# Later loads paced at even distances and a newly searched instruction order in a sparse-attention and gated-FFN kernel

## Chip, cores and metric

The kernel runs on one core of a Trainium2 chip. The metric is device time of one execution in microseconds; three runs of the kernel before took 208.0, 208.16 and 208.38, so its median is 208.16 us. A profile is taken of a further execution.

## What is computed

Block-sparse attention (the mask keeps the window, the first and last blocks, and three drawn blocks for each query block) for 4 batches of 8 heads, 768 tokens of 64 values, and behind it a feed-forward layer whose hidden values are gated by a convolution over three tokens:

```python
scores = scale * np.matmul(q, k.transpose(0, 1, 3, 2))
...
scores = np.where(mask, scores, -1000000000.0)
...
return np.matmul(attn, v).astype(np.float32)      # (4, 8, 768, 64)
...
h = np.maximum(x @ w_in, 0.0)                     # x: (4, 768, 512), w_in: (512, 1024)
...
for k in range(K):
    conv_out += conv_w[k][None, None, :] * hp[:, k:k + S, :]
gate = 1.0 / (1.0 + np.exp(-conv_out))
return (h * gate @ w_out).astype(np.float32)      # w_out: (1024, 512)
```

## The kernel before

**Work.** The 32 heads are taken as 16 pairs, four to a batch. Scores are made transposed, keys on the partitions, in blocks of 128 keys by 128 queries; the mask rides along as 24 extra rows of the contraction (so 88 rows), which is why a pair's slot `t` holds 64 rows of queries and keys and 24 of mask. Eight blocks are one *unit*: score matmuls into a two-bank tile `st` of which there are two (L762), one exponential of 1024 columns on ScalarE into `pt` (L774), and eight matmuls of 65 columns that add up attention times V and its sum in `av` (L799). There are 144 units, 18 for each half of a batch. A pair is thus needed from a known unit on, and comes back in the second half of its batch.

**Behind the scores.** For each half batch and pair, VectorE takes the reciprocal and scales (L707, L709) into `xtok`; a crossbar turn (a transposing DMA on the SP queue, L718) or, at the first and the last pieces, a PE transpose (L728) makes `xT`. The first FFN product (L896) goes through `mix` banks, and is evicted with ReLU into `hE` by ScalarE (L916) or VectorE (L918). The convolution is three products and two sums on VectorE (L954, L962), or for one piece on PE (L973); tanh on ScalarE (L1001, L978) and two more VectorE operations (L1004, L1009) make the gated values `gT`. The second product (L831) is evicted into `o2s` by either engine (the copy helper: L327 on ScalarE, L331 on VectorE) and written out on the SP queue (L840). There are two `mix` banks, and PE's transposes use them too.

**Loads.** Pairs 1 to 5 are loaded by POOL's queue (L239) as natural rows `nat` and `nq` and turned by PE transposes, copied into `t` by the helper. From pair 6 on, K and Q land in `nat`, two crossbar turns on SP (L597) bring them to the staging tile `stg`, and two VectorE copies of 64x1536 bring these into `t` (L331, tile `t<-stg`). V lands in `vn` and is copied to `vt`. Only two staging tiles, four `nat` and three `vn` exist, so a load waits for the copy that empties its buffer.

**Pacing.** POOL would issue every load as soon as a buffer is free. For pairs 8 to 15 a one-element POOL copy (`pace`, L407) reads a corner of the exponential of a chosen unit, so that POOL's queue, which works in order, goes on only once that unit is done. `PACE_U(P)` (L412) gives the unit for K; in `kq_crossbar` and `v_pair` the loads of Q and V follow some units later. Loads of pairs 4 to 7 and of the weights follow each other at a fixed number of loads (L673).

**The order.** Nothing is scheduled when the kernel is built. `Graph` collects 1787 operations, each with its possible engines; `ORDER`, a string of two characters for each operation, one for the engine where there is a choice and one for each buffer that it takes, gives the order in which they are put down, and so the order on every engine and queue. Each engine works through its part in order; waits come from the data and buffers alone.

Of the kernel before, what the change touches and what calls it, by code (L numbers as in the profile page):

```python
# [21 lines left out]
1K11H00l0m0n0o0p0q0Y0Z10V1FA01LA1h0/A1BA1JV0+1GV0r0s0t0u11V1d16V1IA5805910v18V0w0x0y1M05a05b1NV1O01/1262h12j32k  # L22
2v20z0A0B0C0D0E1SA05e05f5j1195g11V15k0F1Y05c05o05p5d0G5l21WV11ZV1+V1XV5q35h0H5t15u0I0J5i5m5C05D5v45H15I2702a1
5E55J05M05N5n5r5s5w5R11b24V11a28V22cV2bV29V5S0K1k15x15F1l1s2iV25y05O15T25+05/5G5K5L5P603631642l0680695Q5U2o1654
5z6d16e6a56f02mV35V2nV2qV2pV5A06i06j1P1610626k16r16s6t25BV01c5W11RV662001QV6w06x676b6c6g5X6y36B16C5Y16h6l6D46G0
6H6I51o1j2wV31n1t6n221V2d22x24S2y5ZV6o6m16u6v6z22V6P16Q6A6E6F6U06V6J6K4T1u6p12r34U2J04V1v2L06R06L06M6W16Z16+6S0
6T6N04W2M4X1w6qV720734Y2X16/27436OV2e1ih0ii4Z1x4+2Z14/2+501y6X1r2KV41p2fV1q2gVijA00771787f07947gik0il6Y707k17h5
7l7m051in1717p07q7r1imViF0iGiHiIio75767u17vipV17w2iq0iriJiK2z17C07D7a7b1isV2AV42BV7H17i7j7I7n7o7s2s0iN17c1iO7E3
7J47t7M07N2C12tV2uViP2EV2DV7x7y7z2iQ7R17S7O57T0iz0iA1z523427AiLiBV27W0537Xit182183iu7F17G7Y1842870887diw0ix7K
8c1iR893ivV37LiS8diyViM02N12OV07P8h08i142PV8e42Q07Q7UiV27V7Z8j53008p18q8r0iW7+085868a3635437557e18u08v8b8fiC1  # L30
8z18A8w1iD2/1317/0iY80382812RV2SViTiXiUiEV8B28g8E08F8k8l8s132V8m18J18K8G3391jf08R08S7B8t8x8y8L48T58W18X8C8D8H8I
8Y08/090911j9194195j138n8oiZj22YV033Vj3j4j58Mjg8N08Ui+962i/8O0j08P3a9c08V8Q28Z8+92939djaj697989h19i9e3jbjhj7992
j89j59a159m09njijc9r19s9o1jdA0jjV13cV3bV3f3g23d0562F03i9w09t41m35V1jo0jpjl1jqA9xjm9y09E13h573o9FjnVjJ0jKjLjMjN
3eV2ju0jv9G29J09K9f19g9k9ljwA9O19p9q9P9L32G1jr02IV2HV9Q59u9T09vjs9UjtV9/19z9A0a03r3s02T13u3p13tjO9V1jR1jS9B1jP
jUjT9CjV9Hjx1jy9IjA0jBa14jzAa40a5jCA2U12VVa919MjZ2a60jW9N9Raaae0jD0jE2WVj+jXafab2ag39SjG1jH9W9Xa21jFA3DjIAaj1ak
ar0a3jQk0j/9Y09Za7a8acaskj0adahal1jYje9b3k03w19D3lkv1aw1ax3j33v4aik1at4k2aB0aCk53k7k6k8k9ay0kwam3E13A3B23Gk3k4
aD5kakbkc9+3xan0kkauavazaAaG1aHaEaFaO0aPklkxaI23nVaQ3aT1aUaV1kmkyknV2ao23yVapaJaY0aZkzA3a+4b11aKb23mVkB0kCkE1kF
kDV14kGVkZ0k+aL1l0aM3F3P3Q33M3S3N03qV33CV4b35b60b7b80be1aR1kK0bfaSbg23R3X3Y1kH1aWkLkMAbj0kIbkaXa/kJA5l51b0b4b5
b93zVbo1bpk/bb0l6l7kN0kObl3bt0bul8bcl1bq1kPA6bv4kQ1bB1kRbCba0bhkW0bibG0bmbHkSAld2lelfbD5bnbrbsbwbxkXbL1bE1bI0l2
aq03I0kojk3T1aN3J3H0bdkAbFbMbN2kYVby2lgbz3OV0lhl9l3l41bQ0kT1bA3UbRkUkVA7ll3lmbJkp0bKbS3bV1bWkqkrksc10c2bObX1la  # L40
bPbTbUbYc61kd1kec7kfbZ0lic343ZV1lnljlolplblklcktA0kgcb0c4ccc5c85cg1c9lqkhA2cd0lrls3+chci2lz0lAlBlClt13LV3KVco0
cpct1culDV1cq3lF0lGb+1b/lHV3VV13WV3/2434041cv1lucy0czlI0lJcD1cacEcecflvcA4cI0cJlKVm10m3m2cjckcl0m4m5cF5cK0lL0lw
lxA3cQ1cRcmcr1cslMlNVlO1lPcV0cWm6cwcxcBcCcGcS3cX1cHc+1c/m7d04lR0cLd30d4lQVm91mamcmb4c4d042d55cN2mdlU1lVlSlTAdb1
cM0lWVm8cOdclX1dg0cTcUlYdhmh2milZVmemkmfmjl+0l/dd0cYcZdl1dm494h4ed1d2d6di2kuc01440cn4a24f4i1dq0drm0AmgmD1d7de1
dn3lEcPdv1dwmx0dfds1dx5dD0dEdjmEdI1dkdodpdtdudJ4q4r14vmlmp3mqmr45msd81mmmtmnd9dF0dymydN0dOdz0dG4gmumodadK2dA0mv
mwdBmFmzdP3dS1dTmAd+046V2d/dU1dHdLdMdQdRdV4se05mBA0e31e44EmG48dC2e80mHV14jdWe9e11e2e50ea34F3mY0mV14n4o04Jed1ee
mWei0ef1dX2dY4bV2mZ47Veje6e7ebeceq1egmXV08m+Vnh0nieherek54tn21nknj4G4u4Bes4ev0ewn3m/04C14kV3n4Vex0eA1eBelem0n0
eteC3eueF0eGn81eH1eN1n9eOen1eon1V9np1nqnsnrntn50n6eS0eTeynaAne1eP4n7Aanx2ezeDeEeIeJeU2lymImCeK0eLnueX1eQ1nfngA
eYf00f14pV34lVnb0ncnyndVbnlnAnF3nHnz4w04mmJ1mKmLmMeRnvepdZkieMf20eZ3nmnBnneVf50f6mNA3mP0fd1eWfef71ff4nGnIno0nJ
4xnwnCe+mQe/mRmSfi0mTA1fjo61o7fk24H4I4P4Q2o30nKnDnEo8AnLfn1o4o5A4yV4fofs0ftfp5fu3ot14zVouov4DA44RV0nMf3f4f8fa1  # L50
f90fgfhnT1flfmnN0nUfA1fBfF0fGnOnVowoxnWfH0fC1nPfK0fqfLnQoyfM4fbnXV0frfvfP1fQfw4K14Lo01nRV24MV04NVfx2fR2ozoAnZ0
n+n/Ao1fU0fVg01g1fD1oc0fEfIfJodo2Aol0omonooopfW5g50g6g23o91oaoeAg71oqobVoB2oDfyoroCosoi0oEga1gbfNfOojfSgf0gc04A
ggof1ogfTgn1fXfY0gog3g4okAohAoR0fZ0nYnSmUoFgh4oX1g8g9gdgp2oJ3f+gs0gtgx1gegigjgq1gyoGoKoLoMoN4Ofc0f/fzoSgu5oYgG0
grgvgz3oHgHgwgAgBgL1gk1oOoIgMgI1oToZgloPoQgN0gQ0gRoUoVA0o+gZ1g+o/V2p70gJ0p8p9papbV1gC0g/4gS2h21gDgmpg1h3phpd0pe
h45h70h8pfA1cpiVh93pm1pnhg1pj0poApkhhgE1gKhl0gOhmgPgTgUh01plAdpB1pCpDpEps0ptpJ0pFgFV1gV2hi1hn0oWp0mOpcpuApGh1h5
hq1pp1pqpKgWpLpMpNprAehrhs2pv0pwpR2pShz0gX1h6hahbhc1hdhj0hAhkhohE1pOgYAhphFhtp11pxAfpPpTpUhB4he0huhv0hfAhG5pHpV
hwp2p3p4py0pI1pzpQhN0p5A0hC1hx1hOhDhHhW1hXhyVqk1pAApWqlhP3hY1qq0qrh/0i0hI0hQhRqmAgpZ3p+pXhJ2q0p/hKq1qsAhq51i81
qB1pYhL0i9qCq2hMA2q6qh0q3hS1qDqEq4hTi10ia2hZ1h+q7qiq8qjAii2i30ibicqn0qFqR0q9A2i40i5i61i7AqoqpAjqGqb1qchU0qt2qu
id2qvhVAqdqwieif0qJ3qKqMqHqxigAqeri0rjqfA3rkAqLqSqyqzr91rarbArA1rBrf0rgrl0rmqArhArc1rdr30qIr4rn2rC1reAqNqOroqT
rpqUqPqQrq0rv1rrrs2rtqVrurR0rL1rwrF1rx3r5rGrSrDryrErzrMrNrOqWrTqaqgp6qXqYr6r7V1rUrPA2rQrVArWr8rHrIrJA3rKqZ0q+q/  # L60
# [53 lines left out]
def kernel(  # L114
# [290 lines left out]
    def pace(u, prio):  # L405
        box = []
        o = op("pace", {"POOL": 0.12}, lambda e: nc.gpsimd.tensor_copy(  # L407
            out=pace_t, in_=pt_t[box[0].index][0:1, 0:1]), prio)
# [649 lines left out]
```

## Time and profile before

| | before |
|---|---|
| runs | 208.0, 208.16, 208.38 us |
| profiled execution | 207.8 us, its span 206.0 us |
| TensorE granted clock | 1.00 throughout |
| read from and written to HBM | 23.09 MB, 6.29 MB |
| DMA, mean over the span | 124 GB/s |

The profile names engines PE (TensorE matmuls), PEld (its weight loads), DVE (VectorE), ACT (ScalarE), POOL and SP. A line of the chain or of the timeline gives start and length in us from the span's start, then engine, tile and source line; an arrow in brackets names what ended the idle time before an instruction. A line of a stretch gives, for each engine, busy us and instructions, then clock, DMA share and GB/s. A line of a wait gives us in total, times, and the longest. Ends of matmuls are modelled, and an engine's durations overlap a little, so distances between starts are the better measure of a rate.

### The profile page before, as it was taken

The numbers are of one execution on the slowest core, as the hardware profiler recorded it, in microseconds if no ns is written. First come the engines' busy times: TensorE is split into PE (matmuls) and PEld (weight loads), VectorE is DVE, ScalarE is ACT, GpSimd is POOL, SyncE is SP. The second block draws the span as 40 slices with busy tenths as digits, with TensorE's granted clock in tenths as the row PEclk, the third lists the DMA queues.
The fourth block names the chain that finished last, engine by engine and source line by source line (L and its number), as shares of the span: only waits on it lengthen the run. The fifth ranks groups of instructions, "written<-read, shape, count | busy, mean of one in ns | idle before, by whom it ended". The sixth has DMA issues, their size and how long they took to land.

```text
span 206.0 us, 6234 instructions
## 1 busy us (share of the span) xinstructions
PE 199.0 (97%) x2409; PEld 142.7 (69%) x2409; DVE 186.3 (90%) x572; ACT 190.5 (92%) x253; POOL 60.7 (29%) x113
## 2 busy tenths in 40 slices
...
GB/s 140 214 196 168 199 154 136 165 123 88 164 129 181 79 191 67 233 149 165 89 59 121 147 110 104 241 149 187 5 165 19 38 175 51 3 2 42 114 28 179
DMA packets 50969, 25.59 MB, mean 124 GB/s; under 512 B 36764, under 2 KB 47996, under 8 KB 50940
## 3 DMA queue, kind: packets, MB, share of 16 engines
...
q14 instruction: 10, 0.08, 0.2%
HBM read 23.09 MB, written 6.29 MB: 143 GB/s over the span
## 4 chain that ended last, share of the span: by engine, by line
PE 76%; ACT 14%; DMA 3%; issue 3%; DVE 2%; SPq 1%; ACTq 0%
PE st L762 26%; PE mix L896 17%; PE mix L831 16%; PE av L799 14%; ACT pt L774 9%; DMA m<-in_v_dram 3%; ACT m L1001 1%; ACT o2s L327 1%; ACT hE L916 1%; PE st L831 1%; PE mix L728 1%; PE mix L522 1%; PE av L973 1%; PE mix L460 1%; DVE t L331 1%
## 5 line engine op out<-in xcount | busy, mean ns | idle before, releaser
L774 ACT ACTIVATE pt<-st 128x1024 bf16<-128x1024 f32 (+1 forms) x145 | 140.2, 1033 | 3.2 <-PE st L762 2.5
L762 PE MATMUL st<-t 88*128 88x256 bf16 (+2 forms) x600 | 91.2, 268 | 1.8 <-DVE t L331 0.9
L762 PEld LDWEIGHTS <-t 88*128 88x128 bf16 x600 | 48.4, 97 | 21.4 <-issue 1.9
L799 PEld LDWEIGHTS <-pt 128*128 128x128 bf16 x1152 | 51.4, 97 | 10.5 <-ACT pt L774 0.2
L799 PE MATMUL av<-vt,pt 128*128 128x65 bf16 x1152 | 57.0, 193 | 0.0
L896 PE MATMUL mix<-xT,winb 128*128 128x384 bf16 (+2 forms) x288 | 54.4, 307 | 0.4 <-ACT o2s L327 0.3
L954 DVE TENSOR_SCALAR m<-hE,cw 128x382 bf16<-128x382 bf16 (+2 forms) x192 | 50.3, 320 | 0.9 <-ACT hE L916 0.6
L831 PE MATMUL mix<-woutb,gT 128*128 128x512 bf16 x184 | 48.5, 379 | 0.0
L962 DVE TENSOR_TENSOR m<-m 128x764 bf16<-128x764 bf16 (+2 forms) x64 | 34.0, 533 | 0.6
L896 PEld LDWEIGHTS <-winb 128*128 128x128 bf16 x288 | 24.7, 97 | 10.2 <-issue 1.3
L1001 ACT ACTIVATE m<-m 128x764 bf16<-128x764 bf16 (+2 forms) x32 | 26.5, 831 | 0.6 <-DVE m L962 0.5
L831 PEld LDWEIGHTS <-gT 128*128 128x128 bf16 x200 | 17.3, 97 | 11.6 <-DVE gT L1009 0.3
L407 POOL COPY pace<-pt 1x1 bf16<-1x1 bf16 x24 | 7.3, 306 | 51.6 <-ACT pt L774 51.5
L916 ACT ACTIVATE hE<-mix 128x384 bf16<-128x384 f32 (+2 forms) x39 | 18.9, 503 | 0.7 <-PE mix L896 0.4
L709 DVE TENSOR_TENSOR xtok<-av,rcp 128x384 bf16<-128x384 f32 (+2 forms) x36 | 18.2, 506 | 0.4
L1009 DVE TENSOR_TENSOR gT<-m,hE 128x764 bf16<-128x764 bf16 (+3 forms) x36 | 18.1, 511 | 0.4
L239 POOL DMA_DIRECT2D nat<-in_q_dram x23 | 17.7, 769 | 1.6 <-issue 1.1
L918 DVE TENSOR_SCALAR hE<-mix 128x384 bf16<-128x384 f32 x25 | 13.7, 552 | 1.0 <-PE mix L896 0.5
L331 DVE COPY t<-mix 64x384 bf16<-64x384 bf16 (+1 forms) x33 | 13.3, 410 | 0.6
L239 POOL DMA_DIRECT2D nat<-in_k_dram x15 | 11.6, 776 | 3.8 <-DMA nat<-in_k_dram 1.8
L1004 DVE TENSOR_SCALAR m<-m 128x764 bf16<-128x764 bf16 (+3 forms) x36 | 12.0, 337 | 0.6 <-ACT m L1001 0.5
L331 DVE COPY o2s<-mix 128x512 f32<-128x512 f32 x9 | 6.2, 688 | 6.5 <-PE mix L831 6.4
...
## 6 DMA issues: line engine op xcount, KB each, us to landing
...
nat<-in_k_dram POOLq DMA_DIRECT2D x15, 192.0 KB, 4.7
vn<-in_v_dram POOLq DMA_DIRECT2D x15, 192.0 KB, 5.8
nat<-in_q_dram POOLq DMA_DIRECT2D x6, 192.0 KB, 5.0
...
```

Of the source, the lines that this page charges most:

```text
L239: return op(name, {eng: occ}, lambda e: on(e).dma_start(out=dst(), in_=src), prio, deps, dma=(kind, service), **kw)
L331: nc.vector.tensor_copy(out=dst, in_=src)
L709: nm = op("norm", {"DVE": t_dps(128 * C)}, lambda e: nc.vector.tensor_tensor(out=xtok_t[xk.index][:, 0:C].rearrange("p c h d -> p h c d"), ...
L762: nc.tensor.matmul(out=st[:, 128 * x:128 * (x + n_)], lhsT=t[0:88, 12 + 6 * hh + kc, :], rhs=t[0:88, idx:idx + (n_ - 1) * (2 if P < NPE el ...
L774: nc.scalar.activation(out=pt_t[ptb.index][:, c0:c1], in_=st_t[stb.index][:, c0:c1], func=AF.Exp, bias=0.0, scale=0.125)
L799: nc.tensor.matmul(out=o[:, off:off + 65], lhsT=pt_t[ptb.index][:, 128 * x:128 * x + 128], rhs=V_t[vslot_b[P].index][:, hh, kc, 0:65], sta ...
L831: nc.tensor.matmul(out=acc(), lhsT=gT_t[gb.index][:, ffc, 128 * t:128 * t + 128], rhs=woutb[:, ffc, c0:c1], start=(ffc == 0), stop=(ffc == ...
L896: nc.tensor.matmul(out=mix_t[hb.index][:, w1 * y:w1 * y + w1], lhsT=winb[:, fc, 128 * ffc:128 * ffc + 128], rhs=xT_t[xt_buf[n].index][:, f ...
L916: nc.scalar.activation(out=dst, in_=src, func=AF.Relu, bias=0.0, scale=0.5)
L954: nc.vector.tensor_scalar(out=m_t[cb.index][:, x, y, 0:w], in0=hE_t[heb.index][:, f0 + y, t0 + x:t0 + x + w], scalar1=cw[:, x, f0 + y:f0 + ...
L962: nc.vector.tensor_tensor(out=m[:, a_, :, 0:w], in0=m[:, a_, :, 0:w], in1=m[:, b_, :, 0:w], op=ALU.add)
L1001: th = [op("tanh", {"ACT": t_act(2 * w) + 0.04}, lambda e, cb=cb, w=w: nc.scalar.activation(out=m_t[cb.index][:, 0, :, 0:w], in_=m_t[cb.in ...
```

## The change

The order string is replaced as a whole. The operations are the same ones, and each keeps its meaning; 28 of them change between ScalarE and VectorE (16 ReLU evictions, 6 output evictions, 2 copies into `xT`, 4 copies and casts of the start). The string was searched with late crossbar turns and late loads among the draws of the search. Beside it, the units that pace the loads of pairs 8 to 15 change: K of the four pairs of a batch at 3, 11, 20, 28 instead of 4, 12, 20, 27 units into the batch before, Q three units behind K instead of two, V six instead of four.

```diff
 ORDER = """
-0002103040M05060708090a011i0L0S0T1T01U2302510b0c0d0e0f1g0U0W0X12V0V1e1f0N0O13A17V0g0h0i0j0k0P0Q0R1AV21CA1DA1E0
...
+000211g010M030405060708090a0S0T1T01U230251262h12j20U0L0O0N0P0Q0R0b0c0d0e0f0g0h0i0j0k0W1e0V0X12V13A17V1AV30Y1CA
...
 """
...
     def PACE_U(P):
         b, j = divmod(P, 4)
-        return 36 * (b - 1) + ((12, 17, 22, 28) if b == 1 else (4, 12, 20, 27))[j]
+        return 36 * (b - 1) + ((12, 17, 22, 28) if b == 1 else (3, 11, 20, 28))[j]
...
-            pq = pace(PACE_U(P) + 2, due - 12)
+            pq = pace(PACE_U(P) + 3, due - 12)
...
-                pv = pace(PACE_U(P) + 4, due - 9)
+                pv = pace(PACE_U(P) + 6, due - 9)
```

More of the change, by code (lines that the diff above doesn't have):

```diff
@@ L20 @@
 ORDER = """
-0002103040M05060708090a011i0L0S0T1T01U2302510b0c0d0e0f1g0U0W0X12V0V1e1f0N0O13A17V0g0h0i0j0k0P0Q0R1AV21CA1DA1E0
[L22 to L60, printed above, removed]
@@ L61 @@
-r0r1A0r2
+000211g010M030405060708090a0S0T1T01U230251262h12j20U0L0O0N0P0Q0R0b0c0d0e0f0g0h0i0j0k0W1e0V0X12V13A17V1AV30Y1CA
+1DA1f1d1E01K10l1H01FA00Z1LV10V0/A0m0n0o0p0q5805911JV1BV1h1GA1IA0r0s0t0u0v1M05a05b0w0x0y0z0A0B0C0D5e05f1NA0+16V
+1SA05j11V15k0E5g15c05d1Y05l211V18V191WV11XV5o05p5q35h1k15i0F1+V1ZV5t15u0G5m0H5n5C05D1O02k1/12d22x31b1a2v21l24V1
+0I0J5r5v45s4S5E55H15I2702a15M05N5J05O10K5R15S5T25w5x15F5G28V22bV2cV29V5+05/5K5L5P6035y02iV21t5z1o631642l1654680
+692o05Q6d16e5U2mV32nV2pV2qV6a55V5A16i06j6f06106266671c5W12y5BV06r16s6k11u1P06b6c4T2r34U2J04V2L04W1v2M6t26w05X6x
@@ new lines @@
+6y36g2016h6B16C6D46l1RV1QV2wV36m16G06H6u1s1n6v6z5Y06I51p4X1w4Y2X14Z1x4+2Z14/2+501y511z5234222V5ZV21V6n26P16Q6R0
+6A6E6F6U06V6J6K1j6o6L06M6p06W16S06Z16+6T6N16qV6OV1r6/2720732e02fV2gV743ih16X77178iiik07f07g794il1q7k17l7h51i
+ijV002KV47m0in16Y707p07q7r1imViF0iGiHiI71ioipV17u17v7w2iJiq0ir7C075762z1isViK2AV42BV7D7H17I7E32C07a7b17i7j7niN1
+7c17J42s17M07N2tV7o7s7t7x537R17S2DV2uV2EViO147y7O57z2iP7AiQiz1iLiR7T03007W07X7Y17diAit082183iBA2842iu870887F17G
+ivV37K7L2N18938c18d7PiM07Q7U7V2OV02PViw07e1iS312/18h0ixiyV8i7Z7+0852Q17/0iV2iW8e48j58p18q3823j38r0868a8b8f8u08v
@@ new lines @@
+2SViT80iYiX8w18g8k8l8z18A2RV7BiC08s18B28E08FiD8G3iU8J18K8L4iEVj918R08S8tja8x8T58y8C8D8W18H8X8I36254378/090iZi+
+j13jf0jg8Y09112YV0j28m18nj4j333V32Vi/941958M8N08U8V8Z8+92939c09d962j5j01mj63919h19ijh979e498jbj7j89j5ji158O29m0
+9n9r19sjc818ojjA09o1jdA13ajo0jp9w09t29909a35V18P3f3g33cV3bV553i3d0562F057jl1jmjnA9x9E19FjqV3eV2jJ08Q23k09y3ju0
+jv9f09g9J0jKjM9K9G0jLjwVjN9k9l9p3h3o2T13p19q9L49O19Pjr19u2G09T09U9v9z2HV2IV9Q5jO9B19Cjs9/1jx09A19V2jyjzAa0a139D
+9b3r3s0jtVjR1jSjP3w1jUjA1jBa402U0jCA3l9Ha5a91aaa619I9M9NjD1jEae09Raf9Sab42VV2WVaj1jFAjZ2jTjVjQj+ag53u3tjWak9W9X
@@ new lines @@
+jG0a20jH9Y2k09Zj/al0jIAar0a3a7a8kv13Dacasadaw1axjXjYkj0ahat3ay1aB0aiamaCan1auavkk3E13G3Ak1k53k6k7k8k9k29+k3k4
+aD4kaaG1aHao1azaAkwaI5aO0aEaFaPklkx3B23F3M3N0aQ2aT1aUaV0kbkckmknV23nVapaJkyaY0aZb11b2aK3v43xkzA33qV33zV3yVa+3
+b31kE0kFkB1kCb60b7aR0aS3H0aL0be1kDV14kGAkZ0k+k/l0kK0kLbfaWb84kMAbg5kH1kIbj0kJV53I1bkkQ0l1bl2kRkSAbo1kT13P3Q23S
+kAjekobpaXbt0a/bub0b4l2bq03mVaMl51l6bv3kN0kOb5kUl8kPV6ld2bB1bCb9ba1bb2bD1kVA7kW0bG0bHbhkXbI4bibmbnbL1brl73R3XbM
+bcbsbwbxbQ0bRaq03T0jkaNkYAbN5bS2kd1bd3JbE0bFkebV1bWkp0lelfl9lall3c10l3lg3CV4lhkqbJbKkrl41by1lbbObPbX0c2c61lic33
@@ new lines @@
+3UkfkgkhA3bzlmljlolnlplcc7c813OV0bAkslqlk3LVbTbUlz1bYcb0ccbZ1c4cg1lrls3KV3VV13WVcd4ktA1b+0b/c5c9cachci5lAlBcelC
+lDA2co0cpct1cfculI0lF1lGlHVlJlKVm10cjm2m4cq0cv3cy0czm3m5cD1ckcEcA4cF53+3/343403Y141kilt1lL0cr0cl2cmcI0lMlNAcscJ
+lulO0lPcwcQ1cK2cR4c4d0m6lQVm91mam7mbmcm8cS1lvlwcxcV0cWcBcCcG3ZV1c+1c/cHlxA0cX3d04lR0cL42494hd30d4c01441cN1mdcO
+d50lSlU1cM1lTAlVdb1dccTcUmelWVmh2mimfdg0lX0dhl+1mklYl/dd5lZVdl1cYcZdi2d1dmd2d6d7de0m0Adn1cnmjmgku4i0dq0drd80mp3
+d9mrmlmqmsmx0ds3lE4e4fdv1mtdwmD1dfdx4mmmElycP45dD0dEdI1djdkdF5dodpdtdJdudymydN0dadz1dGdHdOmnmudK24q4r1dP1dA2mo
@@ new lines @@
+mFmzdBmvmwdS1dT46V247VdU3mAmBV34a24gd+0d/mGdLe31dMdQe4mHV1e04e52dC24jmY0e80mV1e9mWdRed1dVeemZdW4v4n4s4tea04E4F2
+mXV08m+VdX1nh0njdY4w1ei0n21n3ejm/0n0ef5e10eq1ere2e6e7ebdZmI4o0ek14Jn1A94bV2ev0n50ecewes4ninkn4Anlegehex2np1el
+em1eA1eBeC0en0nq4kV3eonsepn6etn7Aaeun81n9eF0eGeN1eOnaAnx2eyezeDnb0nceH5eS0eEeTeInrnt4lVeP1eJne1eX1eYeQ0eK2eL4u
+4m4xnyndAbeU4eZ2nmnunznfnAmJ0mKeRngVnF3nGnB4pV3f00eVeMmLf1f51eWf6nvnnnHno0f25mP1mQmMfd0fef71mNA2ff4nCnInwnJ4yV4
+mRe+e/fi1mSfjf34zVnDmTA0fn0f4o30o4fk2o5Ao61foo7fs1ftfp54G4Bo8Vot0ounEov4C14H4I4PnKnL4Q2fu3nN0nOf8f91fa1nMnT1ow
@@ new lines @@
+fA0fBnUfgnPfF1nVmC4K0484LoxfbfC04DA4fGfH1oyfhnQnRV1fK0nWflfLnZ0fmnXV3n+fc04RV0oz4MV04NVo01o1fP1fM4fQfU0fqfrfvfV
+fwn/Ao2AfR2oAol1omfx0onfW5oofyopfD0oc0g01g1g23o91fEodg50oeAg6g70oqfInSoafJobVoB2oDoCof0ga1fNgbfOgc1fSoggf0ggoi1
+fTfXfY1ojg3g4g8orohAgh4okAgn1gog9gs0gtoEfZ2osoX0oYgdmOnYfzf+oFoJ3oLgp2oKoMoGmU4A4Ogx1geoHgu5gygigjgq0oR1oSgrgv
+gwf/gG0gHgk1oNoIgz3gloOgL1gMgI0gN1gAoToZgBoPoQoUo+gQ0gC0oVV1gDgRgZ1p71g+gS4g/2p8p9pah20h3h71o/V2h45pbV3gmpd0pe
+pg1phpfV1cpiVh8hg0pm0pnh93poApB0pDpj1pkhhhl1gE0plAdgJ1gKgOgPhmgFA1hi0oWp0hn1pp1ps0gTgUpqh00h1h5pCpEhq0h6ptpFpG
```

6 lines of the change are left out of this document (added).

## The prediction

> **What bounds the kernel now.** I read the page's head first, then the stretches of the span, then the chain of work that ended last, and last the waits of TensorE (PE) with the timeline around each.
>
> ```profile
> span 206.0 us, 6234 instructions
> PE 199.0 (97%) x2409; PEld 142.7 (69%) x2409; DVE 186.3 (90%) x572; ACT 190.5 (92%) x253; POOL 60.7 (29%) x113
> PE 76%; ACT 14%; DMA 3%; issue 3%; DVE 2%; SPq 1%; ACTq 0%
> ```
>
> Three engines are nearly full at once, and PE holds 76% of the chain. A busy share of 97% from modelled ends proves little, so I count PE's work by how fast it starts matmuls when nothing holds it. These pieces of the chain are such runs:
>
> ```profile
> 113.21 0.65 PE mix L896 x4
> 114.11 0.44 PE st L762 x4
> 159.39 0.86 PE mix L831 x4
> 161.27 0.48 PE av L799 x16
> ```
>
> Scores: 144 units at 0.44 = 63.4 us. Attention times V: 1152 matmuls at 0.48/16 = 34.6. First FFN product: the equivalent of 256 matmuls of 384 columns at 0.65/4 = 41.6. Second: the equivalent of 192 of 512 columns at 0.86/4 = 41.3. Together 180.9, and with some 170 short transposes, convolutions and warm-up matmuls (about 10 us, an estimate by columns from the same rows) 191 of the 206. The change leaves every one of them in place, so only the other 15 us can move, some 5 of which lie before the first matmul and behind the last.
>
> A rule weighed here: the Trainium skill (Trainium Kernel Development and Optimization, section Performance Expectations) calls matmul busy time a bad metric and takes weight-load busy time instead. By it PE would have 31% to spare (PEld 69%), some 63 us. The start rate does not bear that out, and the sum below goes by the start rate.
>
> The stretches, with busy time of PE, PEld, DVE, ACT, POOL:
>
> ```profile
> 0.00:10.00 10.00, 7.95 (x63) 6.02 (x64) 8.19 (x34) 6.85 (x12) 7.28 (x16) 1.00 0.91 177
> 10.00:57.00 47.00, 46.48 (x673) 36.25 (x671) 45.36 (x137) 46.99 (x54) 24.58 (x46) 1.00 1.08 155
> 57.00:101.00 44.00, 43.56 (x516) 29.76 (x515) 42.12 (x123) 42.77 (x57) 13.67 (x25) 1.00 0.97 147
> 101.00:145.00 44.00, 43.71 (x523) 30.39 (x522) 40.69 (x115) 42.58 (x53) 15.21 (x27) 1.00 0.94 133
> 145.00:188.00 43.00, 43.00 (x515) 31.06 (x512) 38.73 (x123) 41.62 (x59) 0.00 (x0) 1.00 0.17 55
> ```
>
> From 10 to 57 us ScalarE (ACT) never rests (46.99 of 47): its exponentials set the pace there. Later ACT has 1.2 to 1.4 us idle in each stretch and PE is the fuller one. So an order can gain only where PE visibly waits behind 57 us. The granted clock is 1.00 throughout.
>
> **Where PE waits, and on what.** From 57 to 188 us the largest row of the weight loads' waits, and the answer on the staging tile, say:
>
> ```profile
> PEld L762 <- DVE t L331: 1.4, 3, 0.5
> ```
> ```profile
> who waited for it (us, times):
>   PEld L762: 0.9, 2
> ```
>
> PE stood three times before a score matmul for a VectorE (DVE) copy into slot `t`, twice for copies out of the crossbar staging tile (0.9 us). The whole 1.4 is weight-load idling; what PE loses is less, since a matmul still runs. The transfers themselves appear in no wait of PE or ACT after 10 us; the copies come late because of their place on DVE.
>
> **The change part by part.** All 1787 operations stay. 28 of them change between ACT and DVE, but the counts hardly move: ReLU evictions stay 39 on ACT and 25 on DVE, output evictions 16 and 9; at the start ACT gives up one cast for one more slot copy. So the engines' sums stay, and what counts is position. I compared the two programs' order on each engine around each place where PE waits.
>
> *Place A, 100 us (pair 10 becomes due).*
>
> ```profile
> 98.80 1.27 DVE L331 COPY t<-stg 64x1536 bf16<-64x1536 bf16 x2
> 99.99 0.68 DVE L331 COPY o2s<-mix 128x512 f32<-128x512 f32 x1
> ```
> ```profile
> 98.20 1.89 PE L831 MATMUL mix<-woutb,gT 128*128 128x512 bf16 x8
> 100.13 1.05 PE L762 MATMUL st<-t 88*128 88x384 bf16 x8
> ```
> ```profile
> 98.09 2.00 ACT L774 ACTIVATE pt<-st 128x1024 bf16<-128x1024 f32 x2
> 100.83 1.94 ACT L774 ACTIVATE pt<-st 128x1024 bf16<-128x1024 f32 x2 [0.74 <-PE st L762]
> ```
>
> The two copies end at 100.07 and the scores start at 100.13. Eight matmuls from 98.20 at 0.215 are through at 99.92, so PE loses 0.21; ACT stands 0.74. In the new order the first copy stands two gate instructions earlier, the two copies of pair 11 follow at once, the output eviction at 99.99 goes to ACT just ahead of the starved exponential, and one pair of second-product matmuls moves behind the scores. Last copy to first score then has about half a microsecond of cover. Gain 0.21, PE's loss; the bounds are 0 (something else stops PE at the same spot) and 0.74 (ACT's gap, if ACT were the limit).
>
> *Places B and C, 67 and 58 us.*
>
> ```profile
> 66.81 0.38 PE L762 MATMUL st<-t 88*128 88x128 bf16 x2
> 67.39 0.38 PE L762 MATMUL st<-t 88*128 88x384 bf16 x2 [0.20 <-ACT pt L774]
> ```
> ```profile
> 57.11 1.14 PE L896 MATMUL mix<-xT,winb 128*128 128x384 bf16 x6
> 58.26 0.39 PE L762 MATMUL st<-t 88*128 88x384 bf16 x2
> ```
>
> At B two score matmuls take 0.22, the next pair starts 0.58 after them: 0.36 lost, waiting for an exponential to free the score bank. The new order puts two first-product matmuls (2 x 0.65/4 = 0.33) ahead of that score, in the gap: gain 0.33 (0 to 0.36). At C six matmuls of 0.1625 end at 58.08 and the score starts at 58.26: 0.18 lost, waiting for a staging copy; again two such matmuls stand ahead of it now: gain 0.18 (0 to 0.18). Both are true gains only because that work is PE's own and would come anyway.
>
> *Place D, 143 us.*
>
> ```profile
> 140.64 1.03 PE L831 MATMUL mix<-woutb,gT 128*128 128x512 bf16 x4
> 141.94 0.81 PE L896 MATMUL mix<-xT,winb 128*128 128x384 bf16 x4
> 143.03 0.48 PE L896 MATMUL mix<-xT,winb 128*128 128x384 bf16 x2 [0.28 <-ACT o2s L327]
> ```
> ```profile
> 142.38 0.60 ACT L327 COPY o2s<-mix 128x512 f32<-128x512 f32 x1
> 142.85 1.06 ACT L774 ACTIVATE pt<-st 128x1024 bf16<-128x1024 f32 x1
> ```
>
> PE waits for an output eviction to free a `mix` bank: four matmuls of 0.1625 from 141.94 end at 142.59, 0.44 before 143.03. The block's last matmuls are through at 140.64 + 4 x 0.215 = 141.50, the eviction at 142.98: 1.48 later. In the new order the first group that follows takes the bank of the output block before, evicted well ahead, and the group that needs this eviction's bank stands 1.33 us of PE's work behind the block (two score halves 0.44, two V groups 0.24, four first-product matmuls 0.65). The eviction keeps its place on ACT, so 0.15 of the wait is left: gain 0.29, between 0 (ACT later by as much) and 0.44.
>
> *101 to 131 us: a cost.* Ahead of the exponential of unit 108 the new order has three more ReLU evictions and one more output eviction on ACT than the old.
>
> ```profile
> 132.36 0.49 ACT L916 ACTIVATE hE<-mix 128x384 bf16<-128x384 f32 x1
> 132.74 1.02 ACT L774 ACTIVATE pt<-st 128x1024 bf16<-128x1024 f32 x1
> ```
>
> From start to next start a ReLU eviction holds ACT 0.38 and an output eviction 0.47 (142.38 to 142.85): 3 x 0.38 + 0.47 = 1.61 us more. ACT has 44 - 42.58 = 1.42 idle in that stretch. If all of it can be used, PE waits 0.2 for score banks; if half, 0.9; if none, 1.61. Part of these evictions is taken back by unit 112, so I take 0.40, nearer the first.
>
> *The start.*
>
> ```profile
> 2.09 7.18 DMA m<-in_v_dram
> 9.30 0.83 ACT vt L327
> 10.13 3.67 ACT pt L774 x4
> ```
>
> The load of V for pair 0 lands at 9.27 and releases the steady run of exponentials. The first five SP loads and first four POOL loads stay in order, so it should land when it did. ACT now does a 64x384 slot copy between the second half exponential and this V copy, inside the wait. Worth 0; up to 0.3 either way if the load lands otherwise or the inserted copy ends later than 9.30. Behind it the first loads of later queries move back two to four places on POOL, and nearer keys forward: cover both ways until 20 us.
>
> *Even distances.* For pairs 8 to 15 the load of K is paced one unit earlier (first two pairs of a batch), the same, or one later; Q three units behind K instead of two, V six instead of four, so that the last V of a batch goes out three units later.
>
> ```profile
> POOL pace L407 <- ACT pt L774: 51.5, 15, 8.7
> ```
> ```profile
> xT<-xtok SPq DMA_TRANSPOSE x24, 5.4
> stg<-nat SPq DMA_TRANSPOSE x20, 3.9
> vn<-in_v_dram POOLq DMA_DIRECT2D x15, 192.0 KB, 5.8
> ```
>
> POOL waits 51.5 us for those exponentials already; behind a pace copy stand only the next loads. From the first steady exponential at 10.13 to 188 us 143 units run, 1.24 each: three units are 3.7 us. The new order moves the V copies of most of these pairs later on DVE too, by two to fifteen microseconds of DVE's own work. The crossbar turns take 5.4 and 3.9 us to land (medians). On SP they change places with output writes and with each other, but between the last turn of a half batch and its first reader stands as much of PE's work as before or more (the least is 7.4 us, and 0.15 less at one place). Price 0, under that cover; without it one late V stops DVE, which works in order, and each microsecond late is one lost for the gates behind it.
>
> *The end.* From the last score on, the two orders of PE differ by neighbours changing places; the same four matmul pairs, eviction on ACT and write close both: 0.
>
> Sum: -0.21 - 0.33 - 0.18 - 0.29 + 0.40 = -0.61. The profiled execution took 207.8 us, 1.8 around its span of 206.0, so with the change it would take 207.19; the median of the runs, 208.16, lies 0.36 above that execution, which gives 207.55, say 207.6.
>
> **The rivals.** *ACT falls behind PE from 101 to 131 us (slower).* The 1.61 us find no idle time of ACT, since its gaps there come when PE is late with scores, not when ACT has work waiting. Then the term is 1.61 instead of 0.40, and the evictions that PE needs at D come as much later, which takes that 0.29 away: 207.55 + 1.21 + 0.29 = 209.05. It decides once less than about a third of ACT's 1.42 is usable (1.61 - 0.47 = 1.14 outweighs the gains of 1.01). For it: each unit's scores wait for the exponential two units back, and only two such tiles exist. Against it: the taking back by unit 112, and that ACT has idle time in every stretch from 57 us on.
>
> *Filled gaps open elsewhere (no change).* PE gets 1.01 earlier at A to D, and each time then meets an exponential or a ReLU that is as late as before, since ACT and DVE are over 95% full too: 0 gained, and half of the 0.40 to pay, 208.2 to 208.4. For it: ACT is at 97% from 57 to 101.
>
> *The pacing bites (slower).* A V or Q goes out up to 3.7 us later and misses its place by 1 to 2 us after the crossbar's 3.9: 209 to 210. Against it: the copies moved too.
>
> *The change does not do what it says:* the loads stay bunched because POOL's order, not the pace, holds them. That changes no number here, as no load is waited for.
>
> **How the numbers follow.** Forecast 0.48; ACT behind 0.26; given back 0.17; pacing 0.09. For the same or not, 0.2% is 0.42 us, about what a measurement of this kernel can tell from no change. The forecast's own range is 206.8 to 208.2, mostly faster (0.37), some of it same (0.08) and little slower (0.03). ACT behind is slower (0.25), barely same (0.01). Given back: same 0.11, faster 0.04, slower 0.02. Pacing: slower. So faster 0.41, same 0.20, slower 0.39. Small waits of up to 0.3 each can arise at any of the many reordered places, which widens both ends: 206.7 to 209.6 leaves out about 2 in 10.
>
> **What would show it.** Right: no gap before the scores of pair 10 near 100 us and ACT's 0.74 gone; weight loads' wait for DVE's copies into `t` under 0.7; a wait for an output eviction near 143 us of under 0.3. Wrong: score matmuls waiting for exponentials by more than 1 us between 101 and 131 us; DVE or ACT waiting for a load of V; an exponential's gap that was not there; or the first steady exponential starting outside 9.8 to 10.4.

## The result and the profile after

| | before, beside it | changed |
|---|---|---|
| median of 20 runs each | 208.47 us (208.0 to 210.26) | 207.61 us (207.05 to 208.44) |
| ratio | | 0.9957, 95% interval 0.9941 to 0.9974 |
| profiled execution | 207.8 us, span 206.0 | 207.39 us, span 205.4 |

The change makes the kernel 0.4% faster, and 207.6 was predicted. The reasons are less tidy than the number. Ratios, here and below, leave out three single executions that took over 1.5% more than the fastest of their kernel: 341.37 us (e6, granted clock 0.56), 211.38 (e8) and 211.13 (the kernel before).

First the page of the changed kernel: its span, the busy line (PE shows fewer instructions because some matmul records are missing from this trace), and the chain by engine.

```profile
span 205.4 us, 6237 instructions
PE 197.1 (96%) x2392; PEld 142.3 (69%) x2409; DVE 184.9 (90%) x572; ACT 189.7 (92%) x253; POOL 59.4 (29%) x113
PE 68%; ACT 15%; DVE 12%; issue 3%; ACTq 0%; DVEq 0%
```

PE's share of the chain is 68% instead of 76%, and DVE's is 12% instead of 2%: the chain runs along DVE for a longer part. The stretches, with the same cuts as before (those before 10 and behind 145 us are left out):

```profile
10.00:57.00 47.00, 45.91 (x662) 35.83 (x663) 45.38 (x142) 46.62 (x53) 25.30 (x49) 1.00 1.08 154
57.00:101.00 44.00, 43.58 (x524) 30.44 (x528) 41.48 (x120) 43.78 (x58) 11.92 (x24) 1.00 1.00 145
101.00:145.00 44.00, 43.73 (x512) 30.51 (x515) 40.06 (x116) 42.77 (x55) 14.54 (x27) 1.00 1.00 136
```

ACT is the fuller engine from 57 to 101 us now (43.78 of 44, 42.77 before). Two rows of the weight loads' waits from 57 to 188 us, for the copies into `t` and for the gated values of the second product:

```profile
PEld L762 <- DVE t L331: 0.5, 2, 0.3
PEld L831 <- DVE gT L1009: 0.3, 1, 0.3
```

The wait for copies into `t` fell from 1.4 to 0.5, and no row of PE waiting for an exponential or an eviction is left; the second row is new in this window. To see where time was won I use PE's *lag*: the start of a unit's first score matmul, less the time that all matmuls which stand ahead of it in that kernel's order take at about the start rates of the prediction. The rates used are slightly fast, so every column grows by some 0.015 a unit even where PE loses nothing; what is read is how columns differ. The lag is worked out from the starts of all matmuls, so it stands in an ordinary fence; the last row is the last matmul of the second product.

```
unit   before  changed  e9 (new order, old pacing)  e12 (four more ReLU on ACT)
   8    4.89     4.58     4.83     4.67
  20    6.04     6.22     6.17     6.18
  48    7.17     7.27     7.28     7.23
  60    8.39     7.91     8.29     7.88
  64    8.56     8.50     9.02     8.47
  80    8.88     8.82     9.64     8.79
  84    9.14     8.91     9.81     8.87
  92    9.48     9.06     9.96     9.69
 108    9.92     9.41    10.31    10.53
 116   10.56     9.62    10.52    10.74
 124   10.72    10.00    10.91    10.89
 end   11.88    11.22    12.12    12.07
```

The changed kernel is 0.48 ahead at unit 60, has given it back by unit 64, and wins 0.60 for good between unit 80 and the end.

### The profile page after: what moved, and what is told of

Its sections match the earlier page's. It is cut to its first block, busy times and chain, and to the rows that moved or that the text cites. A ratio compares the mean times of both kernels' runs of the same rounds, so it can differ in the third digit from the quotient of the medians.

```text
span 205.4 us, 6237 instructions
## 1 busy us (share of the span) xinstructions
PE 197.1 (96%) x2392; PEld 142.3 (69%) x2409; DVE 184.9 (90%) x572; ACT 189.7 (92%) x253; POOL 59.4 (29%) x113
## 4 chain that ended last, share of the span: by engine, by line
PE 68%; ACT 15%; DVE 12%; issue 3%; ACTq 0%; DVEq 0%
PE st L762 22%; PE mix L896 15%; PE mix L831 15%; PE av L799 12%; ACT pt L774 11%; DVE m L954 3%; DVE t L331 2%; DVE m L962 2%; ACT m L1001 1%; DVE xtok L709 1%; PE st L831 1%; ACT vt L327 1%; DVE diag L379 1%; ACT hE L916 1%; PE mix L728 1%
## 5 line engine op out<-in xcount | busy, mean ns | idle before, releaser
L774 ACT ACTIVATE pt<-st 128x1024 bf16<-128x1024 f32 (+1 forms) x145 | 142.2, 1051 | 4.2 <-PE st L762 3.7
L799 PEld LDWEIGHTS <-pt 128*128 128x128 bf16 x1152 | 54.0, 97 | 14.2
L799 PE MATMUL av<-vt,pt 128*128 128x65 bf16 x1152 | 60.5, 193 | 0.1
L896 PE MATMUL mix<-xT,winb 128*128 128x384 bf16 (+2 forms) x288 | 55.2, 307 | 0.1
L954 DVE TENSOR_SCALAR m<-hE,cw 128x382 bf16<-128x382 bf16 (+2 forms) x192 | 49.1, 312 | 0.4 <-ACT hE L916 0.2
L831 PE MATMUL mix<-woutb,gT 128*128 128x512 bf16 x167 | 47.2, 379 | 0.7
L831 PEld LDWEIGHTS <-gT 128*128 128x128 bf16 x200 | 17.1, 97 | 10.0 <-DVE gT L1009 1.2
L407 POOL COPY pace<-pt 1x1 bf16<-1x1 bf16 x24 | 6.4, 268 | 54.1 <-ACT pt L774 54.0
L916 ACT ACTIVATE hE<-mix 128x384 bf16<-128x384 f32 (+2 forms) x39 | 19.8, 519 | 0.4 <-PE mix L896 0.2
L327 ACT COPY o2s<-mix 128x512 f32<-128x512 f32 x15 | 9.2, 613 | 3.3 <-PE mix L831 3.2
```

The source lines that it names most:

```text
L774: nc.scalar.activation(out=pt_t[ptb.index][:, c0:c1], in_=st_t[stb.index][:, c0:c1], func=AF.Exp, bias=0.0, scale=0.125)
L799: nc.tensor.matmul(out=o[:, off:off + 65], lhsT=pt_t[ptb.index][:, 128 * x:128 * x + 128], rhs=V_t[vslot_b[P].index][:, hh, kc, 0:65], sta ...
L831: nc.tensor.matmul(out=acc(), lhsT=gT_t[gb.index][:, ffc, 128 * t:128 * t + 128], rhs=woutb[:, ffc, c0:c1], start=(ffc == 0), stop=(ffc == ...
L896: nc.tensor.matmul(out=mix_t[hb.index][:, w1 * y:w1 * y + w1], lhsT=winb[:, fc, 128 * ffc:128 * ffc + 128], rhs=xT_t[xt_buf[n].index][:, f ...
L916: nc.scalar.activation(out=dst, in_=src, func=AF.Relu, bias=0.0, scale=0.5)
L954: nc.vector.tensor_scalar(out=m_t[cb.index][:, x, y, 0:w], in0=hE_t[heb.index][:, f0 + y, t0 + x:t0 + x + w], scalar1=cw[:, x, f0 + y:f0 + ...
```

## The experiments

All were run in five rounds beside the kernel before, whose median was 208.56, 208.49 and 208.4 us in the three series. An interval is some 0.5% wide, so the medians tell a gain of 0.4% from nothing, not from half of it; smaller things are read from the traces.

### Order alone, pacing alone

e1_new_order_old_pace is the changed kernel with the old pacing, e2_old_order_new_pace the old order with the new:

```diff
 e1: against the changed kernel
-  ((12, 17, 22, 28) if b == 1 else (3, 11, 20, 28))
+  ((12, 17, 22, 28) if b == 1 else (4, 12, 20, 27))
-  pq = pace(PACE_U(P) + 3, ...)     pv = pace(PACE_U(P) + 6, ...)
+  pq = pace(PACE_U(P) + 2, ...)     pv = pace(PACE_U(P) + 4, ...)
 e2: the same lines the other way, against the kernel before
 both: some exponentials get another pt buffer in the order string
```

> The new order with the old pacing (K of pairs 8 to 15 at 4, 12, 20, 27 units, Q two and V four units behind). Order theory (the gain is made by where instructions stand on PE, ACT and DVE from 66 units on): ratio to the kernel before 0.996, as the change as a whole (0.9957), since no load was waited for. Pacing theory (the gain comes from transfers that are spread): ratio 1.000.

> The old order of every engine and queue with the new pacing (3, 11, 20, 28, Q three and V six units behind). Order theory: 1.000, at most 0.002 off, if a copy of V that kept its old place meets a later load. Pacing theory: 0.996. Late-load theory (the new pacing needs the new order): above 1.003, with DVE or ACT waiting for loads of V.

e1 took 208.6 us, ratio 1.0006 (0.9982 to 1.003); e2 208.45, ratio 0.9991 (0.9968 to 1.0014). Neither half carries the gain. The theory that the order carries all of it, which was the prediction's ("even distances: price 0"), fell. The trace of e1 shows where the first of the gain goes: it stands with the changed kernel up to unit 48 (0.16 apart) and has lost 1.3 us of PE by unit 52. These are rows of its waits from 54 to 64 us:

```profile
DVE t L331 <- DMA stg<-nat: 1.0, 1, 1.0
PE st L762 <- DVE t L331: 0.7, 1, 0.7
```

The staging copy of pair 7 waits for its crossbar turn. That gave the turn theory of the next series.

### Old half, new half

e3_old_then_new and e4_new_then_old join the two orders at the first score of unit 66:

```diff
 e3, new pacing:  old order up to the scores of unit 66, behind it the rest as the new order has it
 e4, new pacing:  new order up to the scores of unit 66, behind it the rest as the old order has it
```

> The old order up to the score matmuls of unit 66 (78 us), the rest in the new order, new pacing. At that point PE stands equally far in both kernels' traces. Order theory: ratio 0.997, the lead of 0.6 us being made behind it, at 100, 111 and 143 us. Start theory (what ACT does in the first 10 us counts): 1.000.

> The new order up to the score matmuls of unit 66 (77 us), the rest in the old order, new pacing. Order theory: 1.000, although the places at 58 and 67 us, priced at 0.51 us, are mended in it, because that lead was given back by 77 us in the trace of after. If the prices at 58 and 67 us hold to the end: 0.9975. Start theory: 0.996.

e3 took 210.43 us, ratio 1.0081 (1.0048 to 1.0113), e4 209.36, ratio 1.0042 (1.0013 to 1.0071). As times both are of little use, since each loses time where neither parent does: e4 0.73 us of PE at 65 us, e3 twice 0.79 before scores that wait for an exponential, at 143.03 and 151.50. As traces they are of use. Here is PE at 143 us, under the old second half:

```profile
142.11 0.81 PE L896 MATMUL mix<-xT,winb 128*128 128x384 bf16 x4
143.17 0.48 PE L896 MATMUL mix<-xT,winb 128*128 128x384 bf16 x2 [0.25 <-ACT o2s L327]
```

Four matmuls of 0.1625 from 142.11 end at 142.76, and the next starts at 143.17: 0.41 lost, as in the kernel before. The gap at 100 us (0.21) and one at 111.7 us (0.21) are there as well, although the pacing is the new one. From unit 64 to unit 108, where those two lie, e3's lag grows as the changed kernel's does (to 0.02), e4's by 0.38 more, the kernel before's by 0.45 more. The gaps belong to the order.

### Is it pair 7's turn?

On SP's queue pair 7's second turn moves ahead of two turns of `xT`, in e5 under the old pacing, in e6 under the new:

```diff
 SP, 48 to 53 us
   stg<-nat  pair 7, first turn
+  stg<-nat  pair 7, second turn
   xT<-xtok
   xT<-xtok
-  stg<-nat  pair 7, second turn
```

> The new order with the old pacing, as in e1_new_order_old_pace, with one change on SP's queue: the second crossbar turn of pair 7 goes out right behind the first, ahead of two turns of xT, some 2.6 us earlier. Turn theory (at the old pacing the loads of pair 8 and the V and Q loads behind them run across that turn, it lands near 58.3 us instead of before 57.2, and VectorE's copy for pair 7 and 1.2 us of PE wait for it): the 1.2 us are recovered, ratio to the kernel before 0.996 (about 207.5 us), and VectorE no longer waits 1.0 us for stg<-nat between 54 and 64 us. Distance theory (it is the loads' spread as such, over the whole kernel, that is worth the gain): no change from the new order at the old pacing, 1.000 (208.5 us). If the turns of xT that move back are late instead, the first product at 57 us waits and it is 1.000 to 1.003.

> The changed kernel (new order and new pacing) with the same move of pair 7's second turn, 2.6 us earlier. The changed kernel's runs fall in two groups, 13 at 207.05 to 207.72 and 7 at 208.0 to 208.44. Turn theory (the upper group is the executions in which this turn loses its race with the loads): the upper group goes, median 207.3 to 207.4, ratio 0.994 to 0.995. Distance theory or a cause of the groups elsewhere: 207.6 as the changed kernel, 0.996, with both groups left.

e5 took 208.54 us, ratio 0.9997 (0.9974 to 1.002): the wait for the turn is gone from its trace and the time is as it was. e6 took 207.47, ratio 0.9947 (0.9924 to 0.9969), which cannot be told from the changed kernel's 0.9957. The turn theory fell: a late turn costs an execution some tenths, but it is not what the pacing buys. Whether it makes the upper group of the changed kernel's runs (8 of 20 from 207.99 us on) stays open: two of e6's runs still lie there, 208.04 and 208.07, both at a granted clock of 0.99, like four of those eight. A part of what e5 still lost stood in another row of its waits, from 10 to 188 us, which neither the kernel before nor the changed one has:

```profile
ACT pt L774 <- PE av L799: 1.1, 3, 0.5
```

### The buffers that a pace copy holds

An exponential writes one of six `pt` buffers, and a pace copy *reads* one: the order string may not give a buffer out again before the pace copy stands in it. With the pacing changed under a fixed order, the buffers had to be handed out anew, and in e1 and e5 one exponential got the buffer used three exponentials earlier. e9 hands each exponential the buffer that fell free earliest, which keeps four at least between two uses; e10 adds the early turn; e11 does the same to e2.

```diff
 order string, the last character of each exponential (its pt buffer)
-  as in the changed kernel where free, else another
+  always the one that fell free earliest
```

> Again the new order with the old pacing, each engine and queue in the same order as in e1_new_order_old_pace; only the buffers that the exponentials write (six of pt) are handed out anew, each exponential taking the one that fell free earliest, so that none is taken again after fewer than four exponentials. In e1 one was taken again after three, and its trace has three waits of exponentials for av products, 1.1 us in all, that neither before nor after has. Rotation theory (e1 lost its gain to those waits, which the pacing forces only through the buffer that a pace copy holds; the order alone carries the gain): those waits are gone, ratio 0.996 (207.7 us), where the executions that lose pair 7's crossbar turn may keep it at 0.998. Distance theory (the even loads are worth the gain): 1.000 (208.5 us).

> e9_new_order_old_pace_rot with pair 7's second crossbar turn right behind its first, as in e6_after_early_turn. If the order alone carries the gain and the old pacing costs only that turn and the rotation: as e6, ratio 0.995 (207.4 us), and PE's lag by unit 143 within 0.2 us of e6's. If the even loads are worth something beside these two: 0.998 to 1.000 (208.0 to 208.5), and the trace should show a load, a turn or a copy of pairs 8 to 15 waited for.

> The old order with the new pacing, as in e2_old_order_new_pace, with the pt buffers handed out by the same rule (in e2 one exponential took the buffer of the one just before it). If the pacing is worth nothing by itself: 1.000 to 0.998 of before. If it helps by itself: under 0.997. If it needs the new order's later turns and copies: 1.000 or above, with the first product or a copy at 55 to 60 us waiting for a crossbar turn.

e9 took 208.16 us, ratio 0.9998 (0.9979 to 1.0018); e10 208.29, ratio 0.999 (0.9964 to 1.0015); e11 209.05, ratio 1.0014 (0.9984 to 1.0044). So four kernels with the new order and the old pacing lie at 0.999 to 1.0006, and two with both at 0.9947 and 0.9957: the new pacing, with the buffers that go with it, is worth about 0.8 us, but only under the new order. My rotation theory was right about the place and wrong in expecting that the simple rule would mend it. ScalarE in e9, from 59 and from 87.5 us:

```profile
59.14 1.02 ACT L774 ACTIVATE pt<-st 128x1024 bf16<-128x1024 f32 x1
60.43 2.86 ACT L774 ACTIVATE pt<-st 128x1024 bf16<-128x1024 f32 x3 [0.27 <-PE av L799]
...
89.78 1.02 ACT L774 ACTIVATE pt<-st 128x1024 bf16<-128x1024 f32 x1 [0.28 <-PE av L799]
```

and PE behind the first of them, in e9 and then in the changed kernel:

```profile
60.83 0.47 PE L799 MATMUL av<-vt,pt 128*128 128x65 bf16 x10
61.50 0.60 PE L762 MATMUL st<-t 88*128 88x128 bf16 x4 [0.20 <-ACT pt L774]
```
```profile
60.83 0.47 PE L799 MATMUL av<-vt,pt 128*128 128x65 bf16 x10
61.13 0.60 PE L762 MATMUL st<-t 88*128 88x128 bf16 x4
```

The exponentials of units 50 and 73 each start 0.10 us behind the last `av` product that reads their buffer. They took a buffer used five units back (units 45 and 68), because the one used six back (units 44 and 67) is the one that the old pacing's V loads of pairs 8 and 11 read, and stands as taken in the order. The new pacing reads units 45 and 70 there, units 50 and 73 get older buffers, and the same score starts 0.37 us earlier. In lag, e9 loses 0.82 us against the changed kernel by unit 80 and hardly more behind it (0.90 at the end): 0.37 at 61.50 and 0.17 at 90.86, both behind these exponentials, and 0.28 elsewhere, half of it before the second-product group at 76.29, where the changed kernel loses 0.14 and e9 0.29. The cause of this 0.28 stays open. In e1, e5 and e10 units 50 and 73 take a buffer used five units back as well, and the scores of units 52 and 75 lose 0.37 to 0.41 and 0.17 there too, against the changed kernel or e6. No load, turn or copy of pairs 8 to 15 is waited for in e9 or in the changed kernel. The first V's pace copy is another matter than its place in the order:

```profile
55.27 0.21 POOL L407 COPY pace<-pt 1x1 bf16<-1x1 bf16 x1
```

It had read its buffer 5 us before unit 50's exponential started at 60.43. So the pace copy no longer held the buffer on the chip, only in the order; a string with that pace copy a few places earlier might have mended e9. That was not tried, nor a seventh buffer, so that the buffers are the cause is read from the traces and not shown by a run that mends them.

### The gaps mended one by one in the old order

e7 mends only the late gaps of the old order, e8 only the two early ones:

```diff
 e7, old order and pacing
 DVE  98 us:    gates of the third piece
+               t<-stg, one copy of pair 10
                gates of the fourth piece
-               t<-stg, one copy of pair 10
                t<-stg, the other
-               o2s<-mix
 ACT  100 us:
+               o2s<-mix
                exponential of unit 81
 PE   100 us: - mix<-woutb x2       scores of units 81, 82      + mix<-woutb x2
 PE   111.7 us: - mix<-winb x2      score half                  + mix<-winb x2
 PE   143 us: + scores x4           mix<-winb that waits        - scores x4
 e8, old order and pacing
 PE   58 us:  + mix<-winb x2        score half that waits       - mix<-winb x2
 PE   67 us:  + mix<-winb x4        score half that waits       - mix<-winb x4
```

> The old order and the old pacing, with only the late gaps mended: at 143 us two score matmuls stand ahead of the first-product group that waits for the output eviction (0.44 of PE), at 111.7 us two score matmuls ahead of a first-product matmul that waits 0.17, and at 100 us the output eviction goes to ScalarE, a staging copy one gate pair earlier and one second-product matmul pair behind the scores (0.21). Theory that gaps behind 100 us are true gains of PE: -0.82 us, ratio 0.996 (207.7 us). Theory that filled gaps open again elsewhere: 1.000 (208.5). Between them, if only the one at 143 us holds: 0.998.

> The old order and the old pacing, with only the two early gaps mended: at 58 us both halves of a first-product matmul group ahead of the score that waits for the staging copy (0.18), at 67 us two first-product matmuls ahead of the score that waits for an exponential (0.36). As the prediction had it: -0.5 us, ratio 0.9975 (208.0). Theory that ScalarE sets the pace up to about 72 us, so that PE meets the next exponential as late as before: 1.000 (208.5), and PE stands at the same place as before by the scores of unit 64 to 68 (76 to 81 us).

e7 took 208.06 us, ratio 0.9985 (0.996 to 1.001): between the theories, and near half of the 0.82. Its trace, an execution of 208.53, shows why. PE around 143 us:

```profile
142.59 0.81 PE L896 MATMUL mix<-xT,winb 128*128 128x384 bf16 x4
143.24 0.60 PE L762 MATMUL st<-t 88*128 88x128 bf16 x4
143.68 0.81 PE L896 MATMUL mix<-xT,winb 128*128 128x384 bf16 x4
144.60 0.60 PE L762 MATMUL st<-t 88*128 88x256 bf16 x4
```

The gap of 0.44 is closed, but the four matmuls from 143.68 end at 144.33 and the next score starts at 144.60: 0.27 lost again (and 0.18 more at 147.92). ScalarE shows what it waited for:

```profile
143.03 0.60 ACT L327 COPY o2s<-mix 128x512 f32<-128x512 f32 x1
143.50 1.06 ACT L774 ACTIVATE pt<-st 128x1024 bf16<-128x1024 f32 x1
```

The exponential that frees the score bank ends at 144.56. At 100 us nothing is won: the staging copy that went ahead delays a gate, the last two second-product matmuls start 0.16 late for it (100.01), and lag grows by 0.23 from unit 80 to unit 82 where the kernel before has 0.22. From unit 80 to the end this execution keeps 0.15 of the 0.82. Moving PE's work alone, or one copy on VectorE, brings PE to evictions, exponentials and gates that are as late as before.

e8 took 208.11, ratio 0.9977 (0.9954 to 1.0). That is the prediction's 0.9975, and it just reaches no gain. The execution that was profiled took 211.38 us, so nothing is read from its trace. It stays open whether these moves pay in the old order; in the changed kernel, where they stand too, they were given back (below).

### How much rest ScalarE really has

```diff
 e12, against the changed kernel, at the same places of the order
-  DVE  hE<-mix (L918)  four ReLU evictions, 105 to 125 us
+  ACT  hE<-mix (L916)
```

> The changed kernel with four more ReLU evictions moved from VectorE to ScalarE between 105 and 125 us, at the same places in the order: 4 x 0.38 = 1.52 us more on ScalarE, which rests 1.23 us of the 44 from 101 to 145 in the changed kernel. If that rest can be used and VectorE's relief counts for nothing: PE loses 0.3 us or less, 207.5 to 207.9 us, ratio 0.996 to 0.9975, and PE's lag grows by at most 1.1 us from unit 80 to unit 116 (0.80 in the changed kernel). If half of the rest can be used (the rule of the prediction, which put 0.40 on 1.61 us): about 0.9 us, 208.5, ratio 1.000. If none: 1.5 us, 209.1, ratio 1.003.

e12 took 208.19 us, ratio 0.9973 (0.9944 to 1.0002), 0.6 us above the changed kernel. In its trace PE's lag grows by 1.95 us from unit 80 to unit 116, 0.80 in the changed kernel: a price of 1.15 for 1.52 us of ScalarE's work, of which 0.85 is left at the end. The lag of 1.95 is far more than the 1.1 of "the rest can be used"; the price lies a little above that of half. The stretches from 108 us, of the changed kernel and then of e12, say why:

```profile
108.00:116.00 8.00, 7.95 (x108) 5.94 (x107) 7.54 (x25) 8.00 (x11) 1.86 (x4) 1.00 1.04 192
116.00:124.00 8.00, 7.95 (x101) 5.47 (x99) 6.95 (x16) 7.83 (x10) 4.00 (x7) 1.00 1.12 100
```
```profile
108.00:116.00 8.00, 7.66 (x103) 5.64 (x102) 6.42 (x23) 8.00 (x13) 1.74 (x3) 1.00 1.14 189
116.00:124.00 8.00, 7.73 (x94) 5.08 (x92) 7.16 (x18) 8.00 (x10) 4.32 (x8) 1.00 0.85 87
```

ScalarE was full there already (8.00 and 7.83 of 8). Its rest of 1.23 us from 101 to 145 lay elsewhere: 0.41 of it from 101 to 108 and 0.65 from 124 to 132. The four added evictions run at 106.77, 112.34, 115.08 and 126.62 us in e12. Against the changed kernel PE has lost 1.09 by 117 us, behind the first three (1.14 of ScalarE's work), and only 0.04 more by 128 us, behind the fourth, which lies in the stretch with rest. The first lies in a stretch with rest too and is paid for even so: the one gap of ScalarE that the trace of the changed kernel shows there (0.41) ends at 102.81, before it.

```profile
101.00:108.00 7.00, 6.94 (x69) 4.61 (x68) 6.44 (x20) 6.59 (x9) 2.16 (x5) 1.00 0.75 105
124.00:132.00 8.00, 8.00 (x108) 5.97 (x107) 6.57 (x21) 7.35 (x11) 5.10 (x10) 1.00 0.98 154
```

## Why the prediction came out as it did

That the time was right to 0.01 us is luck: the profiled execution was to fall by 0.61 and fell by 0.41 (its span by 0.6), while the medians, each of 20 runs, lie 0.86 apart; the median of before that the sum was set against, 208.16 of three runs, was 0.31 low. Within the sum, errors cancelled.

*Place A, 100 us: right.* Gain 0.21 predicted, 0.17 in lag between units 80 and 84 (before loses 0.26 there, the changed kernel 0.09). PE and ACT in the changed kernel:

```profile
99.47 0.38 PE L831 MATMUL mix<-woutb,gT 128*128 128x512 bf16 x1
99.68 0.83 PE L762 MATMUL st<-t 88*128 88x384 bf16 x6
```
```profile
99.94 0.62 ACT L327 COPY o2s<-mix 128x512 f32<-128x512 f32 x1
100.41 2.00 ACT L774 ACTIVATE pt<-st 128x1024 bf16<-128x1024 f32 x2
```

The scores start 0.21 behind the matmul ahead of them, which is that matmul's own time, and the exponential follows the eviction without its gap of 0.74. A like gap of 0.17 at 111.7 us, which the prediction did not see, is gone too.

*Places B and C, 67 and 58 us: the step that failed.* At B the new order puts four first-product matmuls (0.65) ahead of that score, not two, but no more than the gap of 0.36 can be won. The 0.51 is there at unit 60 (lag 0.48 less) and gone at unit 64. PE in the changed kernel at 72 us:

```profile
71.92 0.28 PE L799 MATMUL av<-vt,pt 128*128 128x65 bf16 x4
72.36 0.38 PE L762 MATMUL st<-t 88*128 88x128 bf16 x2
```

Four products of 0.03 end at 72.04, and the score starts at 72.36. From 57 to 72 us ACT is busy without a break:

```profile
57.00:72.00 15.00, 14.95 (x189) 10.89 (x189) 14.36 (x43) 15.00 (x21) 2.85 (x7) 1.00 1.12 135
72.00:81.00 9.00, 8.80 (x102) 5.78 (x102) 7.75 (x20) 8.98 (x12) 3.94 (x8) 1.00 0.87 118
```
```profile
69.95 1.05 ACT L774 ACTIVATE pt<-st 128x1024 bf16<-128x1024 f32 x1
...
71.22 2.00 ACT L774 ACTIVATE pt<-st 128x1024 bf16<-128x1024 f32 x2
```

If the first of the two exponentials from 71.22 takes 1.05 like the one before it, it is through at 72.27: the score waited for that, 0.32. Another 0.14 goes at 75.77, where a second-product group waits for a gate of VectorE (the row of 0.3 for L831 above). "True gains only because that work is PE's own" is not enough. PE did that work sooner and then stood at the next places where ScalarE and VectorE set the pace. This is the rival "filled gaps open elsewhere", true for this stretch and not for the later ones; its "over 95% full" holds from 57 to 101 us only (VectorE has 40.69 of 44 behind that, 92%).

*Place D, 143 us: right in mechanism, too small.* Predicted 0.29, since the eviction was to keep its place on ACT; the whole 0.44 went. In the changed kernel that eviction starts at 141.73 instead of 142.38, and PE has no gap from 141 to 144 us:

```profile
141.73 0.70 ACT L327 COPY o2s<-mix 128x512 f32<-128x512 f32 x1
```
```profile
141.83 1.14 PE L896 MATMUL mix<-xT,winb 128*128 128x384 bf16 x6
142.81 0.38 PE L762 MATMUL st<-t 88*128 88x384 bf16 x2
143.03 0.49 PE L896 MATMUL mix<-xT,winb 128*128 128x384 bf16 x2
```

About 0.24 came back before a score at 152.70. e7 shows what the same PE move is worth when the evictions stay where they were.

*101 to 131 us, the cost of 0.40: absent.* Lag grows by 0.50 from unit 84 to unit 108, and by 0.78 before. No PE wait for an exponential shows. Three added ReLU evictions fall between 128 and 132.5 us, where ScalarE has its rest (7.35 of 8 from 124 to 132, above), and the exponential of unit 108 does come later, 133.25 instead of 132.74, but PE's new order has other work ahead of the scores that follow. The 0.40 was a guess over a stretch of 44 us; the price is set by the place, 0 here, 1.09 of 1.14 for three evictions of e12 and 0.04 of 0.38 for its fourth. One sign of being wrong did appear, gaps before exponentials that the kernel before does not have (0.41 before 102.81, 0.58 before 127.17); there ScalarE waits for scores while PE is busy (8.00 of 8 from 124 to 132, 6.94 of 7 from 101 to 108), so they cost next to nothing.

*The start: 0, and 0 it is.* The V copy starts at 9.13 and the first steady exponential at 9.96 in the chain, within the bounds. In six profiled executions with the old order of the start that copy began between 8.58 and 9.78 us, in eight with the new one between 9.13 and 9.38, so the 0.17 cannot be put down to the order. In seven of the eight the copy follows ScalarE's own slot copy without a wait for the load, so an earlier landing, as e3's (at 8.58 or before), would bring nothing there.

*Even distances: 0, wrong by about 0.8 us.* As far as loads go the step holds: no load of pairs 8 to 15 is waited for with the old pacing or the new. It overlooked that a pace copy reads a `pt` buffer, so that its unit decides which buffer is missing for the exponentials behind it; 0.54 of e9's 0.82 stands right behind two such exponentials, the rest is open. "The pacing bites" had the sign wrong and the wrong mechanism.

*The end: 0, right.* Lag from unit 143 to the end is 0.70 before and 0.71 after.

So in lag from unit 80 on, where the time was won: 0.17 at A, 0.17 at 111.7 us, 0.44 at D, less 0.24 given back, is 0.54 of the 0.60. The sum had 0.51 too much from B and C, 0.40 of a cost that did not come, and missed the rest.
